# Gated mix of full and windowed attention: B's denominators and A's bounds computed with tokens split over the partition groups, B's tap weights sent early into a ring of three

## The chip, the cores and the metric

The kernel runs on one core of one Trainium2 chip. The metric is the device time of one execution in microseconds (us), as the median of three runs. TensorE is called PE, VectorE DVE, ScalarE ACT, GpSimd POOL and SyncE SP, as in the profile.

## The reference

```python
def _A_ref(x, wqkv, wo):            # H = 32 heads, Dh = 20, S = 2048, D = 640
    q, k, v = split_heads(x @ wqkv)
    p = softmax(q k^T * Dh ** -0.5)
    return merge(p v) @ wo

def _B_ref(x, wqkv, wo):            # window of 8 taps, 2 apart, backwards
    q, k, v = split_heads(x @ wqkv)
    logits = q . k[pos - 2 w] * Dh ** -0.5        # w = 0..7, -1e9 before the start
    return merge(sum_w softmax(logits)[w] v[pos - 2 w]) @ wo

g = sigmoid((x * gate_w).sum(-1))
out = g * A(x) + (1 - g) * B(x)     # both read A's x
```

This is the reference in short form. Everything is bf16 outside; A's attention is 32 heads of 2048 x 2048 scores.

## The kernel before, in words

**A's attention** is cut into 32 groups: one block of 512 queries (`qc`) and four heads (`q`). A group has 64 units, each a 128 x 512 piece of scores (16 blocks of 128 keys, four heads). Line 1477 (`qk`) computes scores of two or three units with row-tiled matmuls into one of two PSUM buffers; line 1500 (`exp`) lets ACT take their exponential, two units (1024 columns) or three (1536 columns) at a time. Line 1545 (`pv`) multiplies with the values, four heads at once in four column groups of PE.

**Rides.** The third bank of a score buffer may hold, instead of a third unit for ACT, a unit that DVE takes over: line 1490 turns it into a base-2 exponent by integer arithmetic (`uD`), line 792 makes three shifted versions of four such units (`eD`), and line 784 has POOL scale the values for each (`vS`). A unit that rides costs ACT nothing and DVE one 512-column operation and its share of line 792. The same banks also serve side work as accumulators.

**Bounds of A.** In place of a maximum over the scores there is an upper bound for each query and head, from absolute values. `gen_qd` projects queries (line 658), takes absolute values (line 666), multiplies them with the keys' maxima (line 680: one or two matmuls into 32 partitions and 512 columns), adds a constant (line 687, `qbnd`, 32 partitions x 512) and sends rows of it by DMA into the query tiles (line 700). That happens 20 times.

**B** goes in eight units of 256 tokens (`gen_bproj`, `gen_b`). Queries, keys and values are projected (line 848). For each of eight taps DVE multiplies queries and shifted keys (line 864), PE sums over each head (line 878), DVE takes the maximum over taps (lines 892 to 900, in `repB`), and ACT takes the exponential (line 907, `eB`, 32 partitions for each of four taps, two halves). Then PE computes the gate of the 256 tokens and the denominators, each repeated on all four groups of 32 partitions (128 x 256); ACT takes a tanh (line 919), DVE the reciprocal (line 922) and the product of both (line 924, `rB`). Line 930 copies the weights of each tap into all four partition groups by DMA, in two buffers `repB`: two sets of transfers are issued after line 924 and after the projection is done, and each later one when DVE has consumed a buffer. DVE multiplies with the shifted values (line 941), PE adds up the eight taps, and line 956 multiplies the sum by `rB`. B's next unit starts its query-key products once all of this is done.

**Order of the work.** The program is written down by a planner in the kernel (`_Sched`): each `T(...)` appends an instruction to its engine's list, with waits for what it reads and overwrites, and with a cost that the planner adds to that engine's clock. Every engine, SP's DMA queue included, works off its list in order. The main loop alternates scores, exponentials and products with the values, and spends what PE time is left before a limit on generators (`gen_...`): projections, bounds, B, output products. The limit is the end of the last exponential plus a `SLACK`, one for short and one for long tiles. `PLAN` changes such settings at given tile numbers: slack, when a ride is taken, priorities. Where PE would be too idle, `filler` (line 1566) adds matmuls with no use for the result. `LAT` holds the latencies that the planner assumes between engines.

Of the kernel before, what the change touches and what calls it, by code (L numbers as in the profile page):

```python
# [50 lines left out]
    0: ((0.3, 0.7), 0.26, 2.5, 1.0, 1.0, -1.0, 0.0, 12.0, 7.0, 9.64, 0.4, 0.5, 4.5, 4.21, 0.0, 0.85, 2, 0.0),  # L51
    20: ((0.3, 0.7), 0.12, 2.5, 6.6, 1.0, -1.0, 0.0, 12.0, 7.0, 9.0, 0.5, 0.5, 4.5, 4.0, 0.0, 0.85, 2, 0.0),
    30: ((0.34, 0.69), 0.26, 2.5, 1.0, 1.0, -1.0, -0.17, 12.0, 6.2, 9.64, 0.64, 0.5, 4.5, 4.21, 0.0, 0.85, 1, 0.0),
    40: ((0.3, 0.7), 0.12, 5.5, 1.0, 1.0, -1.0, 0.0, 10.23, 7.0, 9.0, 0.5, 0.5, 4.5, 4.0, -0.06, 0.85, 2, 0.0),
    50: ((0.34, 0.69), 0.26, 2.5, 1.0, 1.0, -1.0, -0.17, 12.0, 6.2, 7.82, 0.64, 0.5, 4.5, 4.21, 0.0, 0.85, 1, 0.0),
    60: ((0.34, 0.69), 0.22, 2.5, 1.0, 1.0, -1.0, -0.17, 12.0, 6.2, 9.64, 0.64, 0.5, 4.5, 4.21, 0.0, 0.85, 1, 0.0),
    80: ((0.41, 0.6), 0.26, 5.5, 1.0, 1.0, -1.17, -0.17, 13.32, 6.2, 7.82, 0.64, 0.47, 4.5, 4.21, 0.0, 0.85, 1, 0.0),
    90: ((0.3, 0.7), 0.2, 2.5, 6.6, 1.0, -1.0, 0.0, 12.0, 7.0, 9.0, 0.4, 0.5, 4.5, 4.0, 0.0, 0.85, 2, 0.0),
    100: ((0.39, 0.45), 0.26, 5.5, 1.0, 1.0, -0.32, -0.31, 13.32, 7.0, 7.14, 0.64, 0.52, 4.5, 4.21, 0.0, 0.85, 1, 0.0),
    110: ((0.41, 0.6), 0.26, 5.5, 1.0, 1.0, -1.17, 0.11, 13.32, 6.2, 9.16, 0.64, 0.47, 4.5, 4.21, 0.0, 0.85, 2, 0.0),  # L60
    130: ((0.34, 0.69), 0.15, 6.6, 2.5, 1.0, -1.0, -0.22, 12.0, 6.2, 9.64, 0.64, 0.35, 4.5, 4.21, 0.09, 0.85, 1, 0.0),
    140: ((0.3, 0.66), 0.2, 2.5, 6.6, 1.0, -1.0, 0.0, 12.0, 7.0, 9.84, 0.4, 0.5, 4.5, 4.0, 0.0, 0.85, 2, 0.0),
    160: ((0.3, 0.66), 0.2, 2.5, 6.6, 1.0, -1.0, 0.0, 12.0, 7.0, 9.84, 0.4, 0.5, 4.5, 4.0, -0.07, 0.85, 2, 0.0),
    170: ((0.3, 0.66), 0.2, 2.5, 5.5, 1.0, -1.0, 0.0, 12.0, 7.0, 9.84, 0.4, 0.5, 4.5, 4.0, 0.0, 0.85, 2, 0.0),
    190: ((0.26, 0.64), 0.2, 2.5, 6.6, 1.0, -1.0, 0.0, 12.57, 7.0, 7.5, 0.4, 0.5, 4.5, 4.0, 0.0, 0.84, 2, -1.5),
    200: ((0.26, 0.64), 0.2, 2.5, 6.6, 1.0, -1.0, 0.08, 12.57, 7.0, 7.5, 0.4, 0.5, 6.24, 4.0, 0.0, 0.84, 2, -1.5),
    210: ((0.26, 0.64), 0.2, 2.5, 6.6, 1.0, -1.0, 0.07, 12.57, 7.0, 7.5, 0.4, 0.5, 6.24, 4.0, 0.0, 0.85, 2, -1.5),
    230: ((0.4, 0.64), 0.2, 2.5, 6.6, 1.0, -1.0, 0.0, 12.0, 7.0, 9.84, 0.4, 0.5, 4.5, 4.0, -0.07, 0.85, 2, 0.0),
    240: ((0.26, 0.64), 0.2, 6.3, 6.6, 1.0, -1.0, 0.07, 12.57, 7.0, 7.5, 0.4, 0.5, 6.24, 4.0, 0.12, 0.85, 2, -1.5),
    260: ((0.24, 0.49), 0.2, 6.3, 6.6, 1.0, -1.0, 0.07, 13.1, 7.0, 7.5, 0.4, 0.25, 6.24, 4.0, 0.12, 0.85, 2, -1.5),  # L70
    270: ((0.3, 0.7), 0.2, 2.5, 6.6, 1.0, -1.0, 0.0, 12.0, 7.0, 9.0, 0.4, 0.5, 4.5, 4.0, 0.0, 0.85, 2, 0.0),
    280: ((0.4, 0.64), 0.2, 2.5, 6.6, 1.0, -1.0, 0.0, 11.56, 7.0, 9.84, 0.4, 0.5, 4.5, 4.0, -0.07, 0.85, 2, 0),
    290: ((0.26, 0.64), 0.2, 2.5, 6.6, 1.0, -1.0, 0.07, 12.57, 7.0, 7.5, 0.4, 0.5, 6.24, 4.0, 0.0, 0.85, 2, -3),
    300: ((0.24, 0.49), 0.38, 1.0, 6.6, 1.0, -1.0, 0.07, 13.1, 7.0, 7.5, 0.4, 0.25, 6.24, 4.0, 0.12, 0.85, 2, -1.5),
    310: ((0.3, 0.7), 0.2, 2.5, 6.6, 1.0, -1.0, -0.04, 12.0, 7.0, 9.0, 0.4, 0.5, 4.5, 4.0, 0.0, 0.78, 2, 0.0),
    320: ((0.23, 0.49), 0.4, 5.5, 6.6, 1.0, -0.91, 0.07, 13.1, 7.0, 7.5, 0.41, 0.4, 6.24, 4.0, 0.12, 0.85, 2, -1.5),
    330: ((0.27, 0.46), 0.4, 5.5, 6.6, 0.91, -0.91, 0.07, 13.1, 7.0, 7.5, 0.41, 0.4, 6.5, 1.59, 0.08, 0.85, 2, 0),
    340: ((0.23, 0.49), 0.4, 5.5, 6.6, 1.0, -1.24, 0.07, 13.1, 7.0, 7.5, 0.41, 0.4, 6.24, 4.0, 0.12, 0.85, 2, -1.5),
    360: ((0.23, 0.48), 0.4, 2.5, 6.6, 0.6, -0.91, 0.07, 13.1, 7.0, 7.5, 0.41, 0.4, 6.24, 3.91, 0.12, 0.85, 2, -1.5),
    380: ((0.23, 0.48), 0.4, 2.5, 6.6, 0.6, -0.91, 0.07, 8.79, 7.0, 7.5, 0.41, 0.4, 6.24, 1.79, 0.12, 0.8, 2, -3),  # L80
    390: ((0.26, 0.45), 0.4, 2.5, 6.6, 0.6, -0.74, 0.07, 8.79, 6.2, 11.1, 0.52, 0.4, 6.24, 1.79, 0.12, 0.8, 2, -3),
    400: ((0.23, 0.48), 0.4, 2.5, 6.6, 0.6, -0.91, 0.07, 8.97, 7.0, 7.5, 0.41, 0.49, 6.24, 1.79, 0.12, 0.8, 2, -3),
    410: ((0.3, 0.7), 0.2, 2.5, 6.6, 1.11, -1.0, -0.76, 12.0, 7.0, 9.0, 0.4, 0.5, 4.5, 4.0, 0.0, 0.9, 2, -3),
    420: ((0.26, 0.45), 0.4, 2.5, 6.6, 0.6, -0.74, 0.07, 8.79, 6.2, 9.1, 0.52, 0.4, 6.24, 1.96, 0.12, 0.8, 2, -3),
    450: ((0.3, 0.7), 0.2, 2.5, 6.6, 0.6, -1.0, 0.23, 12.0, 7.0, 9.67, 0.4, 0.5, 4.5, 4.0, 0.0, 0.85, 2, 0.0),
    460: ((0.23, 0.48), 0.4, 2.5, 6.6, 0.6, -0.91, 0.1, 8.97, 7.0, 6.93, 0.41, 0.49, 6.24, 1.79, 0.2, 0.8, 2, -3),
    470: ((0.23, 0.48), 0.4, 2.5, 6.6, 0.6, -0.91, 0.07, 8.97, 7.0, 7.5, 0.41, 0.49, 6.24, 1.79, 0.12, 0.77, 2, -3),
    480: ((0.23, 0.48), 0.4, 2.5, 6.6, 0.6, -0.91, 0.08, 8.97, 7.0, 7.5, 0.41, 0.49, 6.24, 1.79, 0.12, 0.77, 2, 1),
    490: ((0.23, 0.48), 0.4, 2.5, 6.6, 0.71, -0.91, 0.28, 8.97, 7.0, 7.24, 0.41, 0.37, 6.24, 1.79, 0.12, 0.77, 2, 1),
    500: ((0.24, 0.53), 0.4, 2.5, 6.6, 0.6, -0.91, 0.07, 10.64, 7.0, 7.5, 0.41, 0.49, 4.29, 1.79, 0.12, 0.77, 2, 0),  # L90
    510: ((0.23, 0.48), 0.4, 2.5, 6.6, 0.71, -0.91, 0.28, 8.97, 7.0, 7.24, 0.41, 0.37, 6.24, 5.61, 0.12, 0.77, 2, 1),
    520: ((0.23, 0.48), 0.4, 2.5, 6.6, 0.69, -0.91, 0.1, 8.97, 7.0, 6.93, 0.41, 0.49, 6.24, 1.5, 0.2, 0.8, 2, -3),
    530: ((0.23, 0.48), 0.4, 2.5, 6.6, 0.53, -0.91, 0.07, 8.97, 7.0, 7.5, 0.44, 0.43, 6.24, 1.79, 0.12, 0.77, 2, -3),
    540: ((0.24, 0.53), 0.4, 2.5, 6.6, 0.6, -1.03, 0.07, 10.64, 7.0, 7.5, 0.41, 0.58, 4.29, 1.79, 0.12, 0.77, 2, 0),
    550: ((0.23, 0.48), 0.4, 2.5, 6.6, 0.69, -0.91, 0.1, 9.78, 7.0, 6.44, 0.41, 0.49, 6.24, 1.5, 0.2, 0.8, 2, -3),
    560: ((0.23, 0.48), 0.4, 2.5, 6.6, 0.69, -0.91, 0.1, 9.78, 7.0, 6.44, 0.47, 0.49, 6.24, 1.5, 0.2, 0.8, 2, -3),
    570: ((0.23, 0.48), 0.4, 2.5, 5.5, 0.71, -0.91, 0.28, 8.97, 7.0, 7.24, 0.54, 0.79, 6.24, 5.61, 0.12, 0.77, 2, 1),
    580: ((0.23, 0.48), 0.4, 2.5, 6.6, 0.69, -0.91, 0.1, 9.78, 7.0, 6.44, 0.47, 0.67, 6.24, 1.5, 0.2, 0.8, 2, -3),
    590: ((0.23, 0.48), 0.4, 2.5, 6.6, 0.67, -0.91, 0.07, 8.97, 7.0, 7.5, 0.37, 0.35, 6.24, 1.79, 0.12, 0.77, 2, -3),
    600: ((0.23, 0.48), 0.4, 2.5, 6.6, 0.69, -0.91, 0.1, 9.78, 7.0, 6.44, 0.41, 0.49, 6.24, 1.5, 0.09, 0.8, 2, -3),  # L100
    610: ((0.23, 0.48), 0.39, 2.5, 6.6, 0.69, -0.91, 0.1, 9.78, 7.0, 10.56, 0.47, 0.49, 6.24, 1.5, 0.2, 0.8, 2, -3),
    620: ((0.23, 0.48), 0.28, 6.3, 5.5, 0.67, 0.29, 0.07, 8.97, 5.5, 7.5, 0.37, 0.35, 6.24, 1.79, 0.12, 0.75, 2, -3),
    630: ((0.23, 0.48), 0.39, 2.5, 6.6, 0.69, -0.91, 0.1, 9.78, 7.0, 10.56, 0.47, 0.49, 5.77, 1.5, 0.1, 0.8, 2, -3),
    680: ((0.23, 0.48), 0.39, 5.5, 6.6, 0.71, -0.91, 0.1, 9.78, 7.0, 10.56, 0.47, 0.49, 4.01, 2.8, 0.1, 0.8, 2, -1.5),
    700: ((0.23, 0.48), 0.39, 6.6, 6.6, 0.69, -0.91, -0.25, 9.78, 7.0, 10.56, 0.47, 0.49, 6.24, 1.5, 0.2, 0.8, 2, -3),
    720: ((0.23, 0.48), 0.28, 6.3, 5.5, 0.67, 0.29, -0.38, 8.97, 5.5, 7.5, 0.33, 0.46, 6.32, 1.79, 0.12, 0.75, 1, 0),
    730: ((0.23, 0.48), 0.39, 2.5, 6.6, 0.69, -0.91, 0.1, 9.78, 7.0, 10.56, 0.47, 0.49, 6.24, 1.5, 0.2, 0.89, 1, -3),
}
WEIGHTS = (1.0, 0.83984375, 0.70703125, 0.59375)
UOFF = 15992.765  # L110
K = len(SHIFTS)

LAT = {"pe": 0.18, "act": 0.06, "dve": 0.08, "pool": 0.1, "sp": 0.1}
SWITCH = 0.11

# [18 lines left out]
class _Sched:  # L136
# [7 lines left out]
    def __init__(self, nc, ctx):  # L144
# [8 lines left out]
        self.bufs = {}  # L153
        self.n = 0
        self.mode = None
        self.busy = []
        self.dma_final = {}

    def ready(self, *keys):
# [26 lines left out]
    def task(self, stream, dur, fn, reads=(), writes=(), dma=False, accum=(), mode="full", nd=1, iss=0.75):  # L186
# [27 lines left out]
        for d in t.deps:  # L214
            d.mark = True
            start = max(start, d.end + LAT[d.stream])
# [1523 lines left out]
```

## Time and profile before

| | |
|---|---|
| median of three runs | 850.85 us (850.76 to 851.32) |
| profiled execution | 850.47 us |
| its span, first to last instruction | 848.7 us |
| granted PE clock over the span | 0.998 |
| POOL busy | 142.0 us |
| DVE waiting for PE's scores to ride (line 1490) | 42.0 us |
| reciprocal of B (line 922), each | 1754 ns |
| bounds on DVE (line 687), 32x512, each | 672 ns |
| tanh of B (line 919), 128x256, each | 436 ns |
| tap transfers (line 930) | 128 issues, 32 KB each |

A row of the profile's groups gives line, engine, operation, what is written and read, shapes and count; then busy time and mean duration of one in ns; then the idle time of the engine just before them, and what ended most of it. Busy time is a union, so overlapping ones count once. A row of waits gives who waited for whom: total us, times, the longest.

### The profile page before, as it was taken

How to read it: one execution, taken by the hardware profiler on the slowest of the kernel's cores; microseconds unless marked ns; L12 is line 12 of the kernel's file. 1: busy time of each engine (PE TensorE's matmuls, PEld its weight loads, DVE VectorE, ACT ScalarE, POOL GpSimd, SP SyncE). 2: the span in 40 equal slices, each digit the busy share in tenths (PEclk: the TensorE clock that was granted, in tenths of full speed). 3: DMA queues.
4: the chain of work that ended last, by engine and by line, in shares of the span. 5: the costliest groups of instructions: out<-in, count | busy, mean ns of one | idle time of the engine just before them, and what ended most of it. 6: DMA issues, size and time to landing. Idle time of an engine off the chain costs nothing.

```text
span 848.7 us, 30119 instructions
## 1 busy us (share of the span) xinstructions
PE 821.5 (97%) x12957; PEld 299.7 (35%) x12957; DVE 716.4 (84%) x1212; ACT 809.6 (95%) x770; POOL 142.0 (17%) x181
## 2 busy tenths in 40 slices
PE   8999999999999999999999999999999999999997
PEld 4432232334333343334334243333332333333233
DVE  7566887889899797989888898989998897999973
ACT  4999999999999999999999999999999999999994
POOL 5031014501122110111100111111011111012110
PEclk9999999999999999999999999999999999999999
DMA  9011212001010010011001011010010001001000
GB/s 314 23 40 42 48 31 73 15 13 33 26 27 22 25 42 20 21 25 27 16 16 37 6 20 44 20 31 11 19 32 20 7 20 41 15 7 40 17 6 33
DMA packets 40889, 28.13 MB, mean 33 GB/s; under 512 B 23732, under 2 KB 39556, under 8 KB 40756
## 3 DMA queue, kind: packets, MB, share of 16 engines
q1 hardware_dynamic: 40756, 26.20, 11.8%
q8 instruction: 103, 1.69, 0.8%
q14 instruction: 30, 0.25, 0.1%
HBM read 11.94 MB, written 2.62 MB: 17 GB/s over the span
## 4 chain that ended last, share of the span: by engine, by line
PE 73%; ACT 14%; DVE 8%; issue 5%; SPq 0%; DMA 0%; DVEq 0%; ACTq 0%
PE score L1477 22%; PE obank L1545 18%; PE side L554 16%; ACT ebuf L1500 13%; PE score L554 8%; PE obank L1566 4%; DVE eD L792 2%; PE score L1566 2%; DVE uD L1490 1%; PE side L878 1%; DVE stage L864 1%; PE score L1193 1%; PE obank L457 1%; DVE oN L767 1%; PE score L680 0%
## 5 line engine op out<-in xcount | busy, mean ns | idle before, releaser
L1500 ACT ACTIVATE ebuf<-score 128x1024 bf16<-128x1024 f32 (+1 forms) x738 | 796.5, 1187 | 17.6 <-PE score L1477 14.7
L1477 PE MATMUL score<-qT,kT 32*128 32x512 bf16 x2048 | 295.0, 384 | 9.9 <-ACT ebuf L1500 6.8
L1490 DVE TENSOR_SCALAR uD<-score 128x512 int16<-128x512 f32 x328 | 220.9, 684 | 45.7 <-PE score L1477 42.0
L792 DVE TENSOR_SCALAR eD<-uD 128x2048 int16<-128x2048 int16 x246 | 174.1, 734 | 3.0 <-PE obank L1545 2.3
L1477 PEld LDWEIGHTS score<-qT,kT 32*128 32x128 bf16 x2048 | 72.9, 91 | 263.9 <-ACT ebuf L1500 105.9
L1545 PE MATMUL obank<-ebuf,vA 128*21 128x512 bf16 x1720 | 160.1, 385 | 4.6 <-DVE eD L792 3.5
L784 POOL TENSOR_TENSOR vS<-vA,vw 128x252 bf16<-128x252 bf16 x82 | 62.9, 769 | 259.7 <-PE obank L1545 259.7
L554 PE MATMUL side<-xT,kvw 128*32 128x256 bf16 (+1 forms) x2470 | 101.7, 281 | 0.7 <-DVE qkvB L848 0.6
L1545 PE MATMUL obank<-eD,vS 128*21 128x512 bf16 x984 | 86.0, 379 | 0.0
L760 POOL TENSOR_TENSOR rcp<-rcp,gA 128x16 f32<-128x16 f32 x31 | 12.3, 395 | 386.6 <-DVE rcp L758 367.2
L554 PEld LDWEIGHTS side<-xT,kvw 128*32 128x32 bf16 x2470 | 58.4, 96 | 34.9 <-issue 16.7
L1545 PEld LDWEIGHTS obank<-ebuf,vA 128*21 128x21 bf16 x1720 | 38.6, 89 | 89.3 <-issue 72.9
L1566 PE MATMUL obank<-xT,zero 128*32 128x512 bf16 x688 | 58.5, 383 | 0.0
L864 DVE TENSOR_TENSOR stage<-qkvB 128x1280 bf16<-128x1280 bf16 x64 | 53.7, 866 | 0.1
L941 DVE TENSOR_TENSOR stage<-qkvB,repB 128x1280 bf16<-128x1280 bf16 x64 | 52.6, 848 | 1.0 <-DMA repB<-eB 1.0
L554 PE MATMUL side<-stage,ident 128*32 128x512 bf16 (+1 forms) x736 | 46.7, 345 | 1.0 <-DVE oB L956 0.5
L848 DVE CAST qkvB<-side 128x512 bf16<-128x512 f32 (+1 forms) x70 | 40.5, 587 | 6.4 <-PE side L554 6.4
L765 POOL TENSOR_TENSOR oN<-oTt,rcp 128x512 bf16<-128x512 f32 x31 | 34.8, 1123 | 2.4
L1566 PE MATMUL score<-xT,ident 128*32 128x512 bf16 x380 | 33.7, 381 | 0.0
L1545 PE MATMUL obank<-uD,vA 128*21 128x512 bf16 x328 | 31.9, 379 | 0.0
L754 DVE STREAM_TRANSPOSE oTt<-obank 128x512 f32<-128x512 f32 x32 | 22.8, 712 | 8.9 <-PE obank L1545 8.6
L1545 PEld LDWEIGHTS obank<-eD,vS 128*21 128x21 bf16 x984 | 24.5, 91 | 15.5 <-issue 1.8
(175 smaller groups left out, 622.8 us busy)
## 6 DMA issues: line engine op xcount, KB each, us to landing
repB<-eB SPq DMA_DIRECT2D x128, 32.0 KB
WqP<-in_A_wqkv_dram SPq DMA_DIRECT2D x16, 160.0 KB
stage<-in_B_wqkv_dram SPq DMA_DIRECT2D x1, 2400.0 KB
oTd<-oN SPq DMA_DIRECT2D x108, 20.0 KB
qT<-dst SPq DMA_DIRECT2D x104, 20.0 KB
out_dram<-outsb SPq DMA_DIRECT2D x12, 160.0 KB
kvw<-in_A_wqkv_dram SPq DMA_DIRECT2D x2, 800.0 KB
oTd<-in_A_x_dram SPq DMA_DIRECT2D x2, 640.0 KB
```

The lines of the kernel that those rows point to most:

```text
L554: ins = e.matmul(o[j:k, :], l[:, j:k], r, start=(first and i == 0), stop=(last and i == n - 1), skip_group_check=True)
L765: T(en, c2, lambda e: e.tensor_tensor(oo, ii, ib, ALU.mult), reads=["rcp", "oTt"], writes=["oN0"])
L784: T("pool", 1.0, lambda e: e.tensor_tensor(vS[:, d % 2, :, :], _ap(vA, (kb * NQ + q) * 4 * DV, [[0, K - 1], [1, 4 * DV]]), _ap(vw, 0, [[1, ...
L792: T("dve", 0.11 + 0.1334 * n, lambda e, k=k, sl=sl: e.tensor_scalar(eD[:, sl % NS, 0:512 * n].bitcast(I16), uD[d % 2][:, 0:512 * n].bitcas ...
L848: t = TB(dvc(n * TOK), lambda e, o=o, i=i: e.tensor_copy(o, i), reads=[("side", b)], writes=[key])
L864: TB(dvc(CN * TOK, 2), lambda e, w=w, ks=ks: e.tensor_tensor(prodB(w), qB[:, :, :], ks, ALU.mult), reads=["qB", "kB"], writes=[("prod", w) ...
L941: TB(dvc(CN * TOK, 2), lambda e, w=w, vs=vs, rr=rr: e.tensor_tensor(prodB(w), vs, rr, ALU.mult), reads=["vB", ("repB", w4 % 2)], writes=[( ...
L1477: ins = e.matmul(o, kT[32 * j:32 * j + 32, q, kb * P:(kb + 1) * P], qT[g % NQT][32 * j:32 * j + 32, :], start=True, stop=True)
L1490: t = T("dve", 0.69, lambda e: e.tensor_scalar(uD[d % 2][:, 512 * i:512 * (i + 1)].bitcast(I16), side[x], UOFF, 0.0, op0=ALU.add, op1=ALU. ...
L1500: exps[s] = T("act", actc(512 * n), lambda e: e.activation(ebuf[s % NE][:, 0:512 * n], score[s % 2][:, 0:512 * n], ACTF.Exp, scale=LN2 / S ...
L1545: ins = e.matmul(obank[32 * j:32 * j + DV, :], v, src, start=(kb == 0), stop=(last and k >= len(lst) - 4), skip_group_check=True)
L1566: ins = e.matmul(o[32 * j:32 * j + 32, :], w[:, 32 * j:32 * j + 32] if best else w[:, :], xT[:, 0, 0:512], start=bool(best), stop=bool(bes ...
```

## The change

- A's bounds: the 512 query columns are split over the four partition groups. Line 680's matmul becomes four column-tiled ones of 128 columns, `qbnd` becomes 128 x 128, and each transfer of line 700 becomes four.
- B's gate and denominators: the 256 tokens of a unit are split likewise, 64 to a partition group (`TQ`). Tanh, reciprocal and product work on 128 x 64. The result `rQ` is put together in `rB[0:32]` by four transfers and copied to the other three groups by three more.
- Tap weights: three buffers (`NR`), and the first three sets of transfers are issued right behind the exponential. One set (instead of two) is issued as buffers come free.
- B's next unit may start its query-key products when PE has read the last of the present unit's value products (`bs`), and the bank behind them waits for the whole unit (`b`).
- The planner: other `LAT` values, a model of DVE and POOL that keeps marked DVE operations and POOL's from overlapping in its clock (`port=True`; it adds no instruction and no wait), other costs of some POOL operations, and a new `PLAN`. The instruction lists of all engines come out in another order.

The core of the diff:

```diff
-LAT = {"pe": 0.18, "act": 0.06, "dve": 0.08, "pool": 0.1, "sp": 0.1}
+LAT = {"pe": 0.22, "act": 0.18, "dve": 0.13, "pool": 0.15, "sp": 0.1}
...
+        port = stream == "pool" and not dma or port
+        if port:
+            for a, b in sorted(self.port["dve" if stream == "pool" else "pool"][-8:]):
+                if a < start + dur and start < b:
+                    start = b
+            self.port[stream].append((start, start + dur))
...
-                        ins = e.matmul(side[b][0:32, :], KMd[:, ff, :], qabs[qq][:, :], start=(k == 0), stop=(k == len(fl) - 1),
-                                       skip_group_check=True)
+                        for j in range(4):
+                            ins = e.matmul(side[b][32 * j:32 * j + 32, 0:P], KMd[:, ff, :], qabs[qq][:, j * P:(j + 1) * P],
+                                           start=(k == 0), stop=(k == len(fl) - 1), skip_group_check=True)
...
-                t = T("dve", dvc(512), lambda e, b=b: e.tensor_scalar(qbnd[0:32, :], side[b][0:32, :], 1.0, STEP * TOP, op0=ALU.mult, op1=ALU.add),
+                t = T("dve", dvc(P), lambda e, b=b: e.tensor_scalar(qbnd[:, :], side[b][:, 0:P], 1.0, STEP * TOP, op0=ALU.mult, op1=ALU.add),
...
-        while not (done.get(("bqk", u)) and (u == 0 or done.get(("b", u - 1)))):
+        while not (done.get(("bqk", u)) and (u == 0 or done.get(("bs", u - 1)))):
...
         done[("bl", u)] = True
+        while u and not done.get(("b", u - 1)):
+            yield ("cond",)
...
+        for i in range(NR):
+            taps(i)
...
-        mms = [(side[b][:, TOK:2 * TOK], gwrep(c), xT[:, c, t0:t0 + TOK]) for c in range(CN)]
-        yield from mm_group(b, mms, ["gwT"] + XT(qc), mmc(TOK), per=5)
-        mms = [(side[b][:, 0:TOK], Rep[:, :], eB[:, hh * TOK:(hh + 1) * TOK]) for hh in range(2)]
-        yield from mm_group(b, mms, ["Rep", "eB"], mmc(TOK), per=2)
+                for j in range(4):
+                    ins = e.matmul(side[b][32 * j:32 * j + 32, TQ:2 * TQ], _ap(gwT, c, [[0, 32]]),
+                                   xT[:, c, t0 + j * TQ:t0 + (j + 1) * TQ], start=(c == 0), stop=(c == CN - 1), skip_group_check=True)
...
+                for j in range(4):
+                    ins = e.matmul(side[b][32 * j:32 * j + 32, 0:TQ], Sel, eB[:, hh * TOK + j * TQ:hh * TOK + (j + 1) * TQ],
+                                   start=(hh == 0), stop=(hh == 1), skip_group_check=True)
...
-        t = TB(TOK * 7.5e-3, lambda e, b=b: e.reciprocal(rB[:, :], side[b][:, 0:TOK]), reads=[("side", b), "tB"], writes=["rB"])
+        t = TB(TQ * 7.5e-3, lambda e, b=b: e.reciprocal(rQ[:, :], side[b][:, 0:TQ]), reads=[("side", b), "tB"], writes=["rQ"])
...
+        T("sp", 2.0 + 0.5 * 4, lambda e: [e.dma_start(rB[0:32, j * TQ:(j + 1) * TQ], rQ[32 * j:32 * j + 32, :]) for j in range(4)],
+          reads=["rQ"], writes=["rB"], dma=True, nd=4)
+        spread = lambda: T("sp", 2.0 + 0.5 * 3, lambda e: [e.dma_start(rB[32 * i:32 * i + 32, :], rB[0:32, :]) for i in range(1, 4)],
+                           reads=["rB"], writes=["rB"], dma=True, nd=3)
...
-        taps(0)
-        taps(1)
+        spread()
...
-            if w4 < 2:
-                taps(w4 + 2)
+            if w4 + NR < 4:
+                taps(w4 + NR)
...
+            if f0 + 2 >= CN:
+                done[("bs", u)] = True
```

A line of `PLAN` before and after; its first pair is the slack behind short and long tiles. In all, 57 lines before and 51 after:

```diff
-    320: ((0.23, 0.49), 0.4, 5.5, 6.6, 1.0, -0.91, 0.07, 13.1, 7.0, 7.5, 0.41, 0.4, 6.24, 4.0, 0.12, 0.85, 2, -1.5),
+    320: ((0.3, 0.64), 0.27, 1.0, 6.3, 0.49, -0.83, -0.1, 11.39, 4.5, 10.86, 0.69, 0.23, 5.37, 4.0, 0.05, 0.61, 2, -3),
```

How the instructions of both kernels count on their engines:

| instruction | before | after |
|---|---|---|
| ACT exponentials of 1024 / 1536 columns | 492 / 245 | 406 / 308 |
| rides (line 1490) | 328 | 311 |
| shifted versions of rides (line 792), four units / three | 246 / 0 | 231 / 3 |
| POOL's scaled values (line 784) | 82 | 78 |
| PE products with values | 3032 | 2981 |
| PE fillers | 1224 | 1008 |
| DMA issues on SP | 545 | 727 |

## The prediction

> **What bounds the kernel now.** I read the page first, parts 1 and 2, then the busy time in three stretches, then the groups with shapes kept apart, then the waits of ScalarE (ACT).
>
> ```profile
> span 848.7 us, 30119 instructions
> PE 821.5 (97%) x12957; PEld 299.7 (35%) x12957; DVE 716.4 (84%) x1212; ACT 809.6 (95%) x770; POOL 142.0 (17%) x181
> ACT  4999999999999999999999999999999999999994
> PEclk9999999999999999999999999999999999999999
> ```
>
> PE looks like the bound, but its 97% holds fillers (line 1566, 1224 matmuls) and the modelled ends of pipelined matmuls. ACT is full in every slice but the first and last.
>
> ```profile
> 0.00:19.90 19.90, 16.95 (x131) 9.63 (x135) 14.40 (x34) 8.11 (x10) 12.27 (x21) 1.00 0.96 308
> 19.90:835.80 815.90, 796.63 (x12666) 286.31 (x12660) 696.88 (x1170) 800.42 (x758) 129.75 (x160) 1.00 0.11 26
> 835.80:848.70 12.90, 7.89 (x176) 3.74 (x167) 5.10 (x9) 1.08 (x2) 0.00 (x0) 0.89 0.15 53
> ```
>
> The middle row runs from the first attention exponential to the last: ACT (fourth pair) works 800.4 of 815.9 us. The 19.9 us of head and 12.9 us of tail are untouched by the change. So the time is 32.8 us plus this stretch, plus 1.8 us outside the span (the profiled execution took 850.47 us; the median is 850.85, 0.4 us above it).
>
> ```profile
> L1500 ACT ACTIVATE ebuf<-score 128x1024 bf16<-128x1024 f32 x492 | 476.5, 1043 | 10.1 <-PE score L1477 8.2 <-ACT ebuf L1500 0.3
> L1500 ACT ACTIVATE ebuf<-score 128x1536 bf16<-128x1536 f32 x245 | 344.3, 1479 | 7.2 <-PE score L1477 6.3 <-ACT ebuf L1500 0.3
> L1490 DVE TENSOR_SCALAR uD<-score 128x512 int16<-128x512 f32 x328 | 220.9, 684 | 45.7 <-PE score L1477 42.0 <-ACT g L744 0.7
> L792 DVE TENSOR_SCALAR eD<-uD 128x2048 int16<-128x2048 int16 x246 | 174.1, 734 | 3.0 <-PE obank L1545 2.3
> ACT ebuf L1500 <- PE score L1477: 14.7, 36, 2.1
> ```
>
> ACT takes the exponentials in tiles of two or three 512-column units; VectorE (DVE) takes 328 of the 2048 units, the "rides". Means hide overlap, so I took start-to-start times of following exponentials off the timeline: at best 904 ns after a two-unit tile and 1331 ns after a three-unit one, 427 ns per unit plus 50 per instruction. The floor is 492 x 0.904 + 245 x 1.331 + 0.5 = 771.3 us. The other ACT work between exponentials stretches 20 gaps by 6.9 us. The rest, 37.5 us, is lateness: the next scores were not there. It is 31.7 us after 492 short tiles (64 ns each) and 5.8 after 245 long ones (24 ns). The idle column shows only 14.7, since many small delays do not open a gap.
>
> **The change, part by part.** All costs are against 850.47. The counts come from the instruction order of both kernels.
>
> Rides fall from 328 to 311: 17 units go back to ACT. Tiles become 406 short and 308 long, and one single unit. The floor is 406 x 0.904 + 308 x 1.331 + 0.5 = 777.5: **+6.1 us**, on the path, since ACT sets the end. Fewer instructions (738 to 715) are already in it.
>
> The gate of B runs on 64 columns instead of 256. Eight tanh of 436 ns, at 0.83 ns a column, lose 160 ns each: **-1.3 us**, on ACT.
>
> DVE: eight reciprocals of 1757 ns; by the 16-column row (243 ns) a column costs 6.3 ns, so 64 take about 546: -9.7. The multiply behind each goes from 425 to about 232 (slope between 256 and 512 columns): -1.5. Twenty bounds read 32x512 from PSUM in 672 ns; 128x128 takes 277 (row of line 1079): -7.9. Seventeen rides at 673 ns busy: -11.4; twelve fewer reuses of 708 and three shortened: -9.0. Together -39.5, 716 to 677 us. DVE is not the bound; this is worth only what it removes of PE's waits.
>
> PE: in issue order a quad of four column tiles takes 216 ns at 512 columns, 109 at 256 and 56 at 128; a score group with its switches costs 105 more on either side. Bounds: 36 matmuls at 216 become 36 quads at 56: -5.8. B's gates and denominators: 56 quads from 109 to about 56 (64 columns are in no row; between 28 and 56, I take 56 because weight loads of four tiles remain): -3.0. Fillers, 1224 to 1008: -11.7. Products with V, 3032 to 2981: -2.8. 23 fewer score groups: about -9.8. The whole PE order between first and last scores adds up to 774.0 us before, 741.5 after. Before, PE had as much in its queue as ACT (771.3); after, 36 us less. This is where a gain can come from. Walking both orders tile by tile with these durations (scores ready 0.5 us after their group starts, a score buffer free when its exponential ends, no other waits) leaves ACT waiting 18.3 us before and 11.4 after. So of the 37.5 measured, about 18.3 is PE's packing and 19.2 is waits on others.
>
> Packing: **-6.9**. Waits: DVE's idle share grows from 16% to 20%; its queueing, as load over idle (84/16 = 5.4 against 80/20 = 4.0), would fall by a quarter, -5.0; if the waits were fixed by data and not by DVE's backlog, 0. I take **-4**, nearer the first, because the PE rows that wait name DVE lines most.
>
> SyncE: 42 bound transfers become 168, and 56 for B's factor are new: 545 to 727 issues. A bound issue takes 0.58 us, so some 106 us more in a queue that issues in order. Who is behind it: qT, oTd and output transfers. A bound set goes from at most 3 to 12 issues, +5.2 us for what follows. The tightest I found is group 2, whose bounds were issued at 64.6 us and whose first scores ran at 77.8: six more issues, 3.5 us, fit. Cost 0; without that cover PE, in order, would stall by the difference. The factor's two hops (four and three issues, 4.1 us, and two landings; the final outputs landed within 2.3 us of their last issue) take about 9 us; from reciprocal to first use (line 956) the eight units had 24 us or more. Cost 0; without cover, at most some 9 us a unit of DVE waiting, with everything queued behind it. SP itself waits twice more per unit (on the product, on the first hop): a few us for the transfers behind, under the same cover.
>
> The early tap transfers gain what was waited for them:
>
> ```profile
> who waited for it (us, times):
>   DVE stage L941: 1.0, 2
> ```
>
> 1.0 us of DVE in the whole run, so 0 on ACT. The new latencies and the port model in the planner issue nothing; they act through the order counted above.
>
> Two rules of the Trainium skill speak against this. "DMA: Bandwidth & Descriptors", Specifications, wants 512 B or more per transfer for line rate; the bounds' rows shrink from 1024 B to 256 B. The page of this run has 23732 of 40889 packets under 512 B and the engines busy for 11.8%. Some 2000 small packets more are a twentieth of that count: by the rule a lower rate on under 1% of the time, by the row 0, as nobody waits. And "TensorE: Matmul & The Clock Gate", Why this matters for your kernels, warns that idle gaps of about 3 us halve PE's clock; fillers fall by 18%. The trace shows 0.998 granted and no wait of a score matmul or its weights above 1.3 us, so I take 0; by the rule one such gap would double PE's work in the next 3.4 us window, up to some 3 us a time.
>
> Sum: +6.1 - 1.3 - 6.9 - 4.0 = -6.1: **844.4 us**.
>
> **Rivals.**
>
> - Only the mix counts: lateness per tile stays 64 and 24 ns. 406 x 0.064 + 308 x 0.024 = 33.4, -4.1. Sum +0.7: 851.2. For it: freed PE and DVE time was not what ACT waited for. Against: 774 against 771 us of queued work leaves no room for any delay.
> - The scores come later after short tiles. The plan lets PE work on longer after a short tile (mostly 0.30 to 0.42 us past the last exponential where it was mostly 0.23). If the third of short tiles that is late (over 50 ns: some 140 of 492, so 115 of 406) gets 0.1 us later, that is +11.5: 850.47 + 6.1 - 1.3 - 4.1 + 11.5 = 862.7; with half of it 857. It decides when short tiles are over 62 ns late on average (the 4.8 us of added ACT work is then not won back). Against: the PE work behind short tiles falls in the order (90th percentile 1292 to 1188 ns).
> - The planner meets the chip better than I count: the new latencies and port times leave gaps where they are needed, lateness falls to 20: 837.8.
>
> **Numbers.** The forecast 844.4 has 0.50, the better fit at 838 0.12, the mix alone 0.14, later scores 0.24. About 0.2% (1.7 us) is what a measurement can tell from no change. Faster 0.62, same 0.13, slower 0.25. The range 837 to 857 leaves out a little below and the upper part of the slow case.
>
> **What would show it.** Floor: 406 and 308 in the two exponential rows, with the same shortest spacing. Tanh near 276 ns, reciprocal near 546, bounds near 277. DVE near 677 us, PE's granted clock still 0.998. Lateness, middle stretch less floor and other ACT work, at 26 to 28 us instead of 37.5. I am wrong if that lateness stays over 33, if a score matmul waits for a qT transfer, or if line 956 waits for the factor.

## The result, and the profile after

The changed kernel takes 841.94 us (median of four runs, 841.16 to 844.02) against 850.9: a ratio of 0.9898, with a 95% interval of 0.988 to 0.9916. The forecast was 844.4. The profiled execution took 841.16 us, 9.3 us less than the one before. The page's head, and the same three stretches as before (to the first attention exponential, to the end of the last, to the end). In a row of stretches the length stands first, then busy time and count of PE, its weight loads (PEld), DVE, ACT and POOL, then the granted clock, DMA's share and GB/s:

```profile
span 839.4 us, 29881 instructions
...
PE 791.8 (94%) x12798; PEld 294.1 (35%) x12798; DVE 675.7 (81%) x1183; ACT 808.2 (96%) x747; POOL 129.9 (15%) x177
```

```profile
0.00:20.30 20.30, 17.35 (x131) 10.08 (x135) 13.87 (x34) 8.12 (x10) 12.28 (x21) 1.00 0.96 309
20.30:826.80 806.50, 767.46 (x12543) 280.91 (x12543) 656.76 (x1141) 799.03 (x735) 117.58 (x156) 1.00 0.11 28
826.80:839.40 12.60, 6.98 (x136) 3.13 (x132) 5.11 (x9) 1.10 (x3) 0.00 (x0) 0.89 0.15 54
```

Head and tail stand (20.3 and 12.6 us), and the granted clock is 1.00 in the middle stretch. ACT's busy time there is 799.0 us where it was 800.4, although the tiles ask for more. The middle stretch lost 9.4 us. Its groups and the waits of ACT:

```profile
L1531 ACT ACTIVATE ebuf<-score 128x1536 bf16<-128x1536 f32 x308 | 432.1, 1501 | 3.8 <-PE score L1508 3.0 <-ACT ebuf L1531 0.3
L1531 ACT ACTIVATE ebuf<-score 128x1024 bf16<-128x1024 f32 x406 | 398.0, 1076 | 5.7 <-PE score L1508 4.6
...
L1521 DVE TENSOR_SCALAR uD<-score 128x512 int16<-128x512 f32 x311 | 210.0, 685 | 56.0 <-PE score L1508 52.4 <-ACT g L749 0.7
```

```profile
ACT ebuf L1531 <- PE score L1508: 7.6, 16, 2.1
```

ACT now waits for scores 16 times in gaps that the profile sees (7.6 us; it was 36 times and 14.7 us). DVE's wait for scores to ride grew by 10 us, which costs nothing: DVE has the time. And PE now runs further ahead of ACT: its score matmuls wait longer for ACT to free a score buffer, before and after:

```profile
PE score L1477 <- ACT ebuf L1500: 6.8, 17, 1.0
PE score L1508 <- ACT ebuf L1531: 22.5, 61, 1.0
```

I took the middle stretch apart as in the prediction: floor (shortest spacing, again 904 and 1331 ns), what other ACT work adds, and lateness (the rest), from the start times of following exponentials.

| us | before | after | difference |
|---|---|---|---|
| floor of the tiles | 771.4 | 777.5 | +6.1 |
| other ACT work between them | 6.9 | 5.4 | -1.6 |
| lateness | 37.5 | 23.6 | -13.9 |
| of it after short tiles, per tile | 31.7, 64 ns | 16.7, 41 ns | -15.0 |
| of it after long tiles, per tile | 5.7, 23 ns | 6.8, 22 ns | +1.1 |
| head and tail | 32.8 | 32.9 | +0.1 |

Floor, other work, lateness, head and tail add up to -9.3, as the spans do; differences are taken before rounding.

### The profile page after: what moved, and what is told of

It is laid out like the page before. It is cut to its first block, busy times and chain, and to the rows that moved or that the text cites. A ratio compares the mean times of both kernels' runs of the same rounds, so it can differ in the third digit from the quotient of the medians.

```text
span 839.4 us, 29881 instructions
## 1 busy us (share of the span) xinstructions
PE 791.8 (94%) x12798; PEld 294.1 (35%) x12798; DVE 675.7 (81%) x1183; ACT 808.2 (96%) x747; POOL 129.9 (15%) x177
## 2 busy tenths in 40 slices
DMA packets 45017, 29.16 MB, mean 35 GB/s; under 512 B 27205, under 2 KB 43685, under 8 KB 44885
## 3 DMA queue, kind: packets, MB, share of 16 engines
q1 hardware_dynamic: 44884, 27.25, 12.5%
## 4 chain that ended last, share of the span: by engine, by line
PE 43%; ACT 39%; issue 12%; DVE 4%; SPq 1%; DMA 0%; DVEq 0%; ACTq 0%
ACT ebuf L1531 38%; PE score L1508 13%; PE side L558 10%; PE obank L1576 10%; PE score L558 5%; PE obank L1597 2%; DVE uD L1521 1%; DVE eD L797 1%; PE score L1597 1%; SPq L705 1%; PE side L1597 1%; PE score L1224 1%; PE obank L461 1%; ACT eB L914 0%; PE side L885 0%
## 5 line engine op out<-in xcount | busy, mean ns | idle before, releaser
L1508 PE MATMUL score<-qT,kT 32*128 32x512 bf16 x2048 | 284.5, 384 | 31.0 <-ACT ebuf L1531 22.5
L1521 DVE TENSOR_SCALAR uD<-score 128x512 int16<-128x512 f32 x311 | 210.0, 685 | 56.0 <-PE score L1508 52.4
L797 DVE TENSOR_SCALAR eD<-uD 128x2048 int16<-128x2048 int16 (+1 forms) x234 | 161.0, 711 | 3.8 <-PE obank L1576 2.5
L558 PE MATMUL side<-xT,kvw 128*32 128x256 bf16 (+1 forms) x2580 | 106.0, 282 | 2.2 <-DVE dst L662 0.9
L789 POOL TENSOR_TENSOR vS<-vA,vw 128x252 bf16<-128x252 bf16 x78 | 53.4, 689 | 275.7 <-PE obank L1576 234.3
L1576 PE MATMUL obank<-eD,vS 128*21 128x512 bf16 x933 | 81.8, 379 | 0.0
L765 POOL TENSOR_TENSOR rcp<-rcp,gA 128x16 f32<-128x16 f32 x31 | 9.8, 316 | 368.1 <-DVE rcp L763 368.1
L869 DVE TENSOR_TENSOR stage<-qkvB 128x1280 bf16<-128x1280 bf16 x64 | 50.4, 826 | 0.2
L1597 PE MATMUL obank<-xT,zero 128*32 128x512 bf16 x560 | 43.6, 382 | 0.0
L772 DVE STREAM_TRANSPOSE oN<-oN 128x512 bf16<-128x512 bf16 x32 | 22.5, 705 | 9.3 <-POOL oN L770 9.0
```

The lines of the kernel that those rows point to most:

```text
L558: ins = e.matmul(o[j:k, :], l[:, j:k], r, start=(first and i == 0), stop=(last and i == n - 1), skip_group_check=True)
L789: T("pool", 0.7, lambda e: e.tensor_tensor(vS[:, d % 2, :, :], _ap(vA, (kb * NQ + q) * 4 * DV, [[0, K - 1], [1, 4 * DV]]), _ap(vw, 0, [[1, ...
L797: T("dve", 0.11 + 0.1334 * n, lambda e, k=k, sl=sl: e.tensor_scalar(eD[:, sl % NS, 0:512 * n].bitcast(I16), uD[d % 2][:, 0:512 * n].bitcas ...
L869: TB(dvc(CN * TOK, 2), lambda e, w=w, ks=ks: e.tensor_tensor(prodB(w), qB[:, :, :], ks, ALU.mult), reads=["qB", "kB"], writes=[("prod", w) ...
L1508: ins = e.matmul(o, kT[32 * j:32 * j + 32, q, kb * P:(kb + 1) * P], qT[g % NQT][32 * j:32 * j + 32, :], start=True, stop=True)
L1521: t = T("dve", 0.69, lambda e: e.tensor_scalar(uD[d % 2][:, 512 * i:512 * (i + 1)].bitcast(I16), side[x], UOFF, 0.0, op0=ALU.add, op1=ALU. ...
```

## The experiments

Theory: the end is set by ACT's floor and its lateness; the change pays by less lateness, because PE's queue is packed less full and its order fits better, and DVE's backlog has a small part in it. Rivals: the shorter DVE operations are the gain by themselves; PE's filler matmuls matter through the clock. All four kernels keep the whole instruction order of the kernel that they start from, so that durations change and order does not. The kernel before took 850.45 us in that session. The ratios given are not quotients of the medians; the two differ by up to 0.15%.

**Fillers cut to an eighth, in the old order.**

```diff
-                ins = e.matmul(o[32 * j:32 * j + 32, :], w[:, 32 * j:32 * j + 32] if best else w[:, :], xT[:, 0, 0:512], start=bool(best),
+                ins = e.matmul(o[32 * j:32 * j + 32, 0:64], w[:, 32 * j:32 * j + 32] if best else w[:, :], xT[:, 0, 0:64], start=bool(best),
```

> The kernel before with its order kept, only that each filler matmul (line 1566) moves 64 columns instead of 512 (its result is never used). PE's queue in the main stretch falls from 774 to 717 us by count. Theory (ACT is late because PE's queue is packed too full): walked tile by tile, ACT's wait for packing falls from 18.3 to 12.6 us, so about 845 us (-5.7). Rival 1 (lateness comes from waits on DVE): no change, 850.9. Rival 2 (the fillers keep PE's clock up): granted clock below 0.99, slower than 853.

Measured: 851.35 us, ratio 1.0001 (0.9989 to 1.0013). By the total, the theory fails, which said 845; the total is what the rival of waits on DVE said. But the granted clock of the profiled run is 0.990, and over all ten runs 0.988 to 0.994, where the 25 runs of the kernel before have 0.998 to 1.000. The rows of these windows, first of the shortened-filler kernel and then of the kernel before, have the columns named above:

```profile
356.00:360.00 4.00, 3.39 (x67) 1.32 (x59) 3.90 (x7) 3.99 (x5) 0.00 (x0) 1.00 0.00 0
...
360.00:364.00 4.00, 3.48 (x47) 0.96 (x50) 3.54 (x9) 3.88 (x4) 0.00 (x0) 0.73 0.02 4
...
797.00:803.00 6.00, 6.00 (x52) 1.27 (x56) 3.61 (x6) 3.57 (x5) 0.89 (x2) 0.57 0.03 7
```

```profile
797.00:803.00 6.00, 5.63 (x83) 1.57 (x75) 5.56 (x10) 5.83 (x6) 1.25 (x2) 1.00 0.05 14
```

The clock falls to 0.73 and 0.57 on average over these windows; in the last one PE gets through 52 matmuls where it did 83, and ACT works 3.57 of 6 us where it worked 5.83. A window laid on the first fall alone shows half the clock:

```profile
361.87:365.27 3.40, 3.40 (x35) 0.64 (x33) 2.39 (x7) 3.03 (x3) 0.00 (x0) 0.50 0.00 0
```

The middle stretch has three such falls, of 3.4, 3.4 and 6.8 us. I compared the same exponential in both traces, one by one (both orders are equal), with the other ACT work left in. Where the scores ran at full clock, 729 of 737, their delays sum to 40.0 us instead of 43.6. Behind slowed scores, eight of them, they sum to 5.0 instead of 0.8. So there are two effects of one size: less packing gave 3.6 us (5.7 expected), the lost clock took 4.1. This split was made after the result, and it moves with the border: counting as slowed what starts up to 0, or up to 1.5 us, behind a fall gives 2.7 to 4.2 us for packing and 3.2 to 4.8 for the clock.

**The same in the new order.**

> The changed kernel with its order kept, each filler matmul 64 columns instead of 512. PE's queue falls from 741.5 to 694.5 us by count. Theory (packing): ACT's wait for packing falls from 11.4 to 8.6 us, so about 839 us (-2.8). Rival 1 (waits on DVE): 841.9. Rival 2 (clock): granted clock below 0.99, slower than 844.

Measured: 843.65 us (838.67 to 844.61), ratio to the kernel before 0.9905 (0.9876 to 0.9935): no different from the changed kernel's 0.9898 by these intervals. The fastest run, which is the profiled one, has a granted clock of 0.986, the others 0.974 to 0.983.

```profile
PEclk9999999899999999999999999999999999999799
```

In the profiled run, at full clock (696 of 714 exponentials), the delays fall from 28.7 to 24.8 us, and 18 behind slowed scores add 2.1. Packing is worth 3.9 us here (2.8 expected). In this run the clock takes back half of that; the other three, at lower clocks, are 4.4 to 5.9 us slower. It is not a faster kernel.

**Short operations in the old order.**

```diff
-        t = TB(TOK * 7.5e-3, lambda e, b=b: e.reciprocal(rB[:, :], side[b][:, 0:TOK]), reads=[("side", b), "tB"], writes=["rB"])
+        t = TB(TOK * 7.5e-3, lambda e, b=b: e.reciprocal(rB[:, 0:64], side[b][:, 0:64]), reads=[("side", b), "tB"], writes=["rB"])
...
-                t = T("dve", dvc(512), lambda e, b=b: e.tensor_scalar(qbnd[0:32, :], side[b][0:32, :], 1.0, STEP * TOP, op0=ALU.mult, op1=ALU.add),
+                t = T("dve", dvc(512), lambda e, b=b: e.tensor_scalar(qbnd[0:32, 0:P], side[b][0:32, 0:P], 1.0, STEP * TOP, op0=ALU.mult, op1=ALU.add),
```

The product and the tanh are cut in the same way; the columns left out hold ones.

> The kernel before with its order kept and the short DVE and ACT operations of the change: reciprocal, product and tanh on 64 of 256 columns, bounds on 128 of 512; the other columns are left out (they hold ones). About 19 us of DVE work and 0.5 to 1.3 us of ACT work less, PE's work unchanged. Theory (the order is what pays, DVE's backlog is a part of it): 1 to 3 us less, about 849. Rival (the shorter operations themselves are the gain): at least 6 us less, 845 or below. If only the order counts: 850.5.

Measured: 849.79 us, ratio 0.9991 (0.9982 to 1.0). The page's head and the reciprocal's row:

```profile
PE 821.1 (97%) x12957; PEld 299.8 (35%) x12957; DVE 699.9 (83%) x1214; ACT 808.6 (95%) x770; POOL 140.3 (17%) x181
```

```profile
L927 DVE RECIPROCAL rB<-side 128x64 f32<-128x64 f32 x7 | 3.9, 555 | 5.3 <-ACT tB L924 5.3
```

DVE's busy time fell by 16.5 us, 716.4 to 699.9. Lateness went from 37.5 to 37.2 us, other ACT work from 6.9 to 6.1. Taking DVE work away where the order does not use it gives next to nothing: the rival (6 us or more) falls for this order. The theory's 1 to 3 us are not reached either, so DVE's backlog falls as a cause of lateness here.

**Long operations in the new order.**

```diff
-    qbnd = sb([P, P], BF16, "qbnd")
...
-    rQ = sb([P, TQ], FP32, "rQ")
+    rX = sb([P, 4 * TQ], FP32, "rQ")
+    rQ = rX[:, 0:TQ]
+    qbnd = rX[:, 3 * TQ:4 * TQ].bitcast(BF16)
...
-                t = T("dve", dvc(P), lambda e, b=b: e.tensor_scalar(qbnd[:, :], side[b][:, 0:P], 1.0, STEP * TOP, op0=ALU.mult, op1=ALU.add),
+                t = T("dve", dvc(P), lambda e, b=b: e.tensor_scalar(rX[:, TQ:4 * TQ].bitcast(BF16).rearrange("p (a c) -> p a c", c=P), sap(b, 0, [[0, 3], [1, P]]), 1.0, STEP * TOP, op0=ALU.mult, op1=ALU.add),
...
-        t = TB(TQ * 7.5e-3, lambda e, b=b: e.reciprocal(rQ[:, :], side[b][:, 0:TQ]), reads=[("side", b), "tB"], writes=["rQ"])
+        t = TB(TQ * 7.5e-3, lambda e, b=b: e.reciprocal(_ap(rX, 0, [[TQ, 3], [1, TQ]]), sap(b, 0, [[0, 3], [1, TQ]])), reads=[("side", b), "tB"], writes=["rQ"])
```

> The changed kernel with its order kept, but the reciprocal runs over 192 columns and the bounds over 384 (each reads its input three times; the extra columns are not used): some 11 us more of DVE work. Theory: 1 to 2 us more, about 843.3. Rival (the shorter operations are the gain): 4 us or more, 846 or above. If only the order counts: 841.9.

Measured: 851.12 us, ratio to the kernel before 1.0002 (0.9992 to 1.0012). That is what the rival said (846 or above), and far from the theory's 843.3: 11.8 us more of DVE work (687.5 against 675.7) cost the whole gain.

```profile
PE 794.2 (94%) x12798; PEld 293.0 (35%) x12798; DVE 687.5 (81%) x1183; ACT 809.6 (95%) x747; POOL 130.3 (15%) x177
```

In this kernel `rQ` names the tile that also holds the bounds; its reciprocal and who waited for it, then the waits for its bounds (line 693):

```profile
L952 DVE RECIPROCAL rQ<-side x8: 1349/1358/1359, 223.4 to 777.6; 128x192 f32<-128x192 f32 x8
...
  PE side L559: 4.7, 6
```

```profile
PEld side L559 <- DVE rQ L693: 4.7, 8, 1.5
```

In the changed kernel PE waits 0.8 us for the reciprocal, three times, and its weight loads 2.4 us for the bounds:

```profile
L951 DVE RECIPROCAL rQ<-side x8: 546/558/559, 223.9 to 769.3; 128x64 f32<-128x64 f32 x8
...
  PE side L558: 0.8, 3
```

Lateness rises from 23.6 to 33.3 us. Compared one by one, the delays lie at a few places. At full clock (708 of 714) they grow by 5.4 us, and six exponentials behind slowed scores add 4.3 us: in the profiled run the clock halves twice for 3.4 us in the middle stretch, and the ten runs have 0.990 to 0.996 where the changed kernel's four have 0.997 to 0.999. Each of the eight units of B has such a place soon after its reciprocal. In five an exponential is 0.70 to 0.81 us later, about the length that the reciprocal gained (1357 against 556 ns is 0.80); in one, two exponentials are 0.36 and 0.32 us later; in the two others one is 1.4 and 1.7 us later, with slowed scores. One place in time order, long operations first, then the changed kernel:

```profile
356.22 1.36 DVE L952 RECIPROCAL rQ<-side 128x192 f32<-128x192 f32 x1 [0.81 <-PE obank L1577]
...
357.73 0.95 PE L559 MATMUL side<-xT,kvw 128*32 128x256 bf16 x28 [0.51 <-DVE rQ L952]
...
358.61 0.39 PE L1509 MATMUL score<-qT,kT 32*128 32x512 bf16 x3
...
359.11 2.79 ACT L1532 ACTIVATE ebuf<-score 128x1536 bf16<-128x1536 f32 x2 [0.75 <-PE score L1509]
```

```profile
354.58 0.56 DVE L951 RECIPROCAL rQ<-side 128x64 f32<-128x64 f32 x1 [0.81 <-PE obank L1576]
...
355.41 0.94 PE L558 MATMUL side<-xT,kvw 128*32 128x256 bf16 x28
...
356.27 0.10 PEld L1508 LDWEIGHTS score<-qT,kT 32*128 32x128 bf16 x3 [0.21 <-issue]
```

The projection behind the reciprocal writes into the bank that the reciprocal still reads. PE works off its list in order, so the scores behind the projection wait as well, and ACT behind them for 0.75 us. In the changed kernel the reciprocal is over 0.27 us before the projection starts.

Together, the last two kernels say this: the shorter operations do next to nothing in an order planned around long ones (0.3 us of lateness), and are needed in one planned around short ones (9.7 us, of which 5.4 at full clock and 4.3 through the clock). In this new order the gain needs both together: with the reciprocal and the bounds at three times their columns it is not faster than the old kernel. Whether the new planner would have found as good an order for the long operations was not measured.

**What was not measured:** the old work under the new planner, the new work under the old planner, and late taps in the new order. So the shares of the planner's new latencies, of its port model, of `PLAN` and of the early taps are not told apart. POOL's operations did get shorter (line 784's scaled values from 769 to 689 ns), but no run shows what that is worth.

## Why the prediction was right, point by point

- **ACT is the bound, and its floor rises by 6.1 us:** borne out, with the spacing and the tile counts that were foreseen (the terms of the floor before add up to 771.4, not 771.3).
- **Tanh, -1.3:** borne out, -1.2. The gaps that hold a tanh went from 2.2 to 1.0 us, most of them from 264 to 104 ns, the 160 that were foreseen; the other 0.4 came from the four that write `g`. The profile's duration of a tanh does not show it: 370 ns, not 276 (281 at the old place, in the experiment).
- **DVE 677 us:** 675.7. Reciprocal 556 ns (546 foreseen), product 225 (232), bounds 282 to 286 (277).
- **Packing, -6.9:** right in kind. Cutting PE's fillers alone moved lateness at full clock by 3.6 us where the tile walk said 5.7, and by 3.9 where it said 2.8. So 6.9 is plausible in size, though it was not isolated in the change itself; that PE's score matmuls wait 22.5 us for ACT's buffers instead of 6.8 speaks for it. Quads of 64 columns follow each other after 29 ns in the changed kernel, not 56: B's gates freed about 1.5 us more of PE than was counted (56 quads).
- **Waits on DVE, -4, because DVE's backlog shrinks:** this step failed. 16.5 us less DVE work in the old order took 0.3 us off lateness. PE's score weights did not wait less for DVE's rides in the changed kernel either (28.1 us against 24.2 before). The rows did not name DVE most: those weights waited 105.9 us for ACT. (And 84/16 is 5.25; 5.4 comes from unrounded shares.) What counted in the experiments is not how busy DVE is but which operation holds a bank that the next PE instruction needs.

```profile
PEld score L1477 <- ACT ebuf L1500: 105.9, 268, 1.3
PEld score L1477 <- DVE uD L1490: 24.2, 55, 1.1
PEld score L1508 <- DVE uD L1521: 28.1, 60, 0.9
```

- **The sum:** lateness -10.9 forecast, -13.9 measured; 23.6 us is below the 26 to 28 that were to show it. Of this 6.9 may be packing; the other 7.0 I can only ascribe to where the new order puts work between banks and engines, since nothing here isolates it. One hint: between the moment when its score buffer comes free and an exponential that is over 50 ns late, PE's idle time covers 3.7 of 32.6 us of delay before and 1.8 of 19.1 after. Modelled ends and earlier waits hide some, so it settles nothing, but it points to PE's order more than to waits. That the total came within 2.5 us is in part luck: 4 us of it stood for a mechanism that did not show, and gains without a term of their own took its place.
- **SP and DMA, 0:** borne out for the score path: no score waits for a query transfer, and line 970 waits 0.1 us in all. Line 987, which multiplies by the factor, waits for PE alone. Packets under 512 B rose by 3473 where my estimate was some 2000, and the hardware queue's share from 11.8% to 12.5%. One wait of DVE is new, 0.9 us on a bound transfer still reading `qbnd`.
- **The Trainium skill on small transfers** ("DMA: Bandwidth & Descriptors", Specifications): it asks for 512 B or more per transfer for line rate. 27205 packets lie under 512 B, and no score, value product or exponential waits for a transfer, so this run puts no price on the rule.
- **The Trainium skill on the clock** ("TensorE: Matmul & The Clock Gate", Why this matters for your kernels): the change itself kept its clock at 0.998, as forecast. The clock does fall close by: with the fillers cut to 64 columns the clock fell, and in the window before the first fall PE was never idle for longer than some 0.5 us. A rule on idle gaps of about 3 us would have let that pass. A stretch at half clock cost less than the 3 us that were set against it: four stretches of 3.4 us took 4.1 us in the old order, six took 2.1 in the new one, two took 4.3 with the long operations.
- **The rivals:** the mix alone (851.2) and later scores (857 and more) are out: short tiles are late by 41 ns, under the 62 at which the sign turns. The better fit (837.8) was not nearer: lateness came to 23.6 where it said 20 and the forecast 26.6, and the time lies 4.1 us above it and 2.5 below the forecast.

## What to carry to other kernels

An operation is worth shortening where the in-order engine behind it needs the buffer that the operation holds, and here only an order made anew used the time. In a kernel with a written order, change durations with the order kept, in both orders: the two answers (here 0.3 and 9.7 us of lateness, the clock's part included) tell where the operation lies on the path, which busy shares don't. Measure a bound engine's lateness as spacing over the shortest spacing; its idle column showed 14.7 of 37.5 us.

## What the runs showed of the hardware

PE's clock can fall while PE is busy most of the time. In the old order with short fillers PE was busy for 3.39 of 4 us by the profile (modelled ends included), with no gap of 1 us, and in the next 4 us the granted clock was 0.73. In all three kernels whose clock fell in the middle stretch it went to one half, for 3.4 us or two or three times that. A quad of 64 columns shows as 0.20 us busy although such quads follow each other after 29 to 39 ns, so the profile's busy share overstates how active the array is. The price in that run was 4.1 us, about as much as the freed PE time had won; the long operations in the new order lost 4.3 us in the same way, where PE's longest idle times ahead of the two falls were 0.7 and 1.2 us.
